# A recurrent attention kernel with its segment loop rebuilt: four column tiles, shared leftover rows, 12 of 32 weight slabs streamed

## The chip, the cores and the metric

The kernel runs on one core of one Trainium2 chip. The metric is the device time in microseconds. The time before is 4046.12 us (median of 3 runs, 4042.35 to 4054.03).

Names used below: PE is the matmul engine (PEld its loads of the stationary operand), DVE the vector engine, ACT the scalar engine, POOL the general-purpose engine; SP only issues DMAs here. A "q" behind an engine's name (ACTq) means its instruction queue. HBM is the memory off the chip. A column tile is a strip of columns of PE's array (32 or 64 here, `tile_position` in the code) with a stationary operand of its own. To evict is to copy a result out of the matmuls' accumulators. The granted clock is the share of full speed that the records give PE; they know only 1.0 (full) and 0.5 (half).

## The reference

The output is the sum of three things over 2048 rows of width 1024. The first is the input itself. The second is a dense block (1024 to 3584 with a gelu, back to 1024) on the normalised rows. The third is attention in segments of 32 rows that carries 8 memory rows along:

```python
for s in range(n_seg):                       # 64 segments, one after another
    xs = x[:, s * seg_len:(s + 1) * seg_len, :]
    h = concatenate([mem, xs], axis=1)       # 8 memory rows + 32 rows
    q, k, v = h @ Wq, h @ Wk, h @ Wv         # 1024 -> 32 heads x 128
    p = softmax(where(mask, q @ k.T * scale, -1e9))
    o = (p @ v) @ Wo                         # 4096 -> 1024
    mem = o[:, :8, :]                        # the next segment needs these
    outs.append(o[:, 8:, :])
```

Each of Wq, Wk, Wv and Wo is 8 MiB in bf16. Neither kernel keeps all 32 MiB on chip (18 MiB before, 20 after); the rest is read again from HBM in each of the 64 segments. The loop is serial: the memory rows of one segment come out of the Wo product of the one before.

One caution on correctness. Every run below agreed with the reference within the comparison's tolerance. So did an experiment that used wrong weights on purpose (`nostream`). The attention term is evidently small beside the other two, so agreement says little about the recurrent part. The experiments other than `nostream` and `fill` change only the order, place or time of the same operations; `fill` adds zeros.

## The kernel before

The dense part keeps all of w1 and w2 on chip and runs in four groups of 512 rows.

The segment loop keeps Wq, Wk and a quarter of Wo on chip. Q and K use the weights as the stationary operand, with 40 moving columns. V uses the 40 rows of `h` as the stationary operand, O the 40 rows of the attention's result, both in two column tiles, with Wv and three quarters of Wo streamed in blocks of 1 MiB:

```python
for i, h in enumerate(range(g0, g1)):                  # Q and K
    for kt in range(KT):
        nc.tensor.matmul(pv[:, i, :], lhsT=W_sb[:, kt, h*DH:(h+1)*DH], rhs=hT[:, kt, :], ...)

for kq in range(KT // 4):                              # V; O is alike
    blk = spool.tile([P, 4, 1024], BF16, name="wblk")
    nc.sync.dma_start(out=blk, in_=Wv_v[...])          # 1 MiB
    for kk in range(4):
        nc.tensor.matmul(psA[0:L, :],     lhsT=hT[:, kt, :], rhs=blk[:, kk, 0:512],    tile_position=(0, 0))
        nc.tensor.matmul(psB[QB:QB+L, :], lhsT=hT[:, kt, :], rhs=blk[:, kk, 512:1024], tile_position=(0, QB))
```

The softmax here doesn't subtract the row's maximum and nothing guards it: scores larger than these inputs give would overflow.

## Time and profile before

| stage | from the trace |
|---|---|
| dense matmuls | 54.6 to 502.5 us |
| 64 segments | one per 54.4 us (mean spacing of the output stores), 14 MiB streamed in each |

First some lines of the page of the kernel before: engines with busy time and share, the granted clock in tenths per fortieth of the span, the DMA share in the same slices, and the chain that ended last.

```profile
PE 3026.4 (75%) x48265; PEld 1854.1 (46%) x48265; DVE 871.5 (22%) x1764; ACT 1020.1 (25%) x1561; POOL 9.9 (0%) x23
...
PEclk9999967777777787777787777777777777777777
DMA  4000097787777777877777787777787777778776
...
PE 55%; DMA 24%; ACT 8%; issue 7%; DVE 6%; SPq 1%; ACTq 0%; DVEq 0%
```

Next, groups of instructions from the same page (line, engine, operation, tiles, shapes, count, then busy us, mean ns and the idle time before them with its releaser), and the line of the largest DMA issue (size of one, us to landing).

```profile
L373 PE MATMUL ps<-wblk,oT 128*40 128x512 bf16 x1536 | 657.0, 578 | 297.4 <-DMA wblk<-in_A_Wo_dram 296.5
...
L266 PE MATMUL ps<-hT,Wk_sb 128*128 128x40 bf16 x16384 | 485.1, 188 | 177.3 <-issue 177.2
...
wblk<-in_A_Wv_dram SPq DMA_DIRECT2D x512, 1024.0 KB, 8.7
```

No engine is full. PE is busy 75% of the span, at a clock of seven to eight tenths in the loop, and 24% of the chain is DMA. A third view gives one stretch of the loop: busy time of PE, its weight loads, DVE, ACT and POOL, then the granted clock, the DMA share and GB/s.

```profile
600.00:4000.00 3400.00, 2531.75 (x45112) 1622.27 (x45108) 653.97 (x1185) 824.16 (x1243) 0.00 (x0) 0.78 0.77 275
```

The queue that feeds the loop has a share of 0.77. In stretches where it is full (share 1.0 and more) it moved 369 to 397 GB/s with 2 KB rows, so about a quarter of its time is lost.

### The profile page before, as it was taken

What the parts mean: (1) busy time and instruction counts of PE and PEld (TensorE: products, weight loads), DVE (VectorE), ACT (ScalarE), POOL (GpSimd) and SP (SyncE); (2) the same over time, 40 slices, a digit from 0 to 9 for tenths busy, and PEclk for the clock granted to TensorE, in tenths of its full rate; (3) what the DMA queues carried; (4) which work ended last, traced back from release to release, by engine and by line L of the source; (5) the groups of instructions that cost most, each with busy time, mean ns of one, the idle gap of its engine ahead of it and who ended that gap; (6) DMA issues with size and microseconds to landing.
All of it is one profiled execution on the core that took longest, in us unless ns stands there. A gap on an engine that the chain in (4) does not pass through costs nothing.

```text
span 4043.0 us, 102945 instructions
## 1 busy us (share of the span) xinstructions
PE 3026.4 (75%) x48265; PEld 1854.1 (46%) x48265; DVE 871.5 (22%) x1764; ACT 1020.1 (25%) x1561; POOL 9.9 (0%) x23
## 2 busy tenths in 40 slices
PE   5999937777777777777777777777777777777777
PEld 2444424444454544444544444445444444544444
DVE  4343302112112211121122111212112112211211
ACT  3333312122222222222222122222122222212222
POOL 0000000000000000000000000000000000000000
PEclk9999967777777787777787777777777777777777
DMA  4000097787777777877777787777787777778776
GB/s 172 32 32 27 12 347 250 272 292 278 269 282 260 276 274 285 296 282 259 282 265 265 277 296 275 264 268 271 262 290 284 277 274 266 263 270 293 281 275 247
DMA packets 502262, 1004.93 MB, mean 249 GB/s; under 512 B 20035, under 2 KB 28227, under 8 KB 499788
## 3 DMA queue, kind: packets, MB, share of 16 engines
q1 hardware_dynamic: 494396, 985.74, 67.8%
q8 instruction: 377, 6.18, 0.6%
q10 hardware_dynamic: 6160, 8.41, 0.6%
q0 software_dynamic: 1280, 4.20, 0.3%
q14 instruction: 49, 0.40, 0.0%
HBM read 985.69 MB, written 12.58 MB: 247 GB/s over the span
## 4 chain that ended last, share of the span: by engine, by line
PE 55%; DMA 24%; ACT 8%; issue 7%; DVE 6%; SPq 1%; ACTq 0%; DVEq 0%
PE ps L266 23%; DMA wblk<-in_A_Wo_dram 18%; PE ps L288 9%; PE ps L373 9%; PE ps L181 4%; DMA wblk<-in_A_Wv_dram 4%; PE ps L154 3%; PE ps L292 2%; PE ps L312 2%; ACT L340 2%; ACT L339 2%; ACT rsum L340 1%; ACT pack L296 1%; ACT rsum L339 1%; DVE pack L387 1%
## 5 line engine op out<-in xcount | busy, mean ns | idle before, releaser
L373 PE MATMUL ps<-wblk,oT 128*40 128x512 bf16 x1536 | 657.0, 578 | 297.4 <-DMA wblk<-in_A_Wo_dram 296.5
L288 PE MATMUL ps<-wblk,hT 128*40 128x512 bf16 x2048 | 595.3, 443 | 138.5 <-DVE hT L247 88.5
L377 PE MATMUL ps<-wblk,oT 128*40 128x512 bf16 x1536 | 664.7, 584 | 0.0
L266 PE MATMUL ps<-hT,Wk_sb 128*128 128x40 bf16 x16384 | 485.1, 188 | 177.3 <-issue 177.2
L292 PE MATMUL ps<-wblk,hT 128*40 128x512 bf16 x2048 | 595.8, 443 | 6.1 <-issue 6.1
L296 ACT CAST pack<-ps 40x512 bf16<-40x512 f32 x256 | 147.0, 574 | 1786.0 <-PE ps L292 1665.3
L266 PEld LDWEIGHTS <-Wk_sb 128*128 128x128 bf16 x16384 | 472.9, 101 | 183.8 <-issue 183.8
L266 PEld LDWEIGHTS <-Wq_sb 128*128 128x128 bf16 x16384 | 442.9, 98 | 149.2 <-issue 149.2
L266 PE MATMUL ps<-hT,Wq_sb 128*128 128x40 bf16 x16384 | 461.6, 183 | 65.8 <-issue 65.8
L377 PEld LDWEIGHTS <-oT 128*40 128x40 bf16 x2048 | 240.8, 134 | 413.3 <-issue 412.8
L373 PEld LDWEIGHTS <-oT 128*40 128x40 bf16 x2048 | 270.0, 136 | 340.6 <-issue 309.0
L288 PEld LDWEIGHTS <-hT 128*40 128x40 bf16 x2048 | 212.1, 111 | 331.0 <-issue 176.2
L297 DVE CAST pack<-ps 40x512 bf16<-40x512 f32 x256 | 177.4, 693 | 547.7 <-PE ps L292 492.2
L382 DVE CAST pack<-ps 8x512 bf16<-8x512 f32 x64 | 43.8, 685 | 934.5 <-PE ps L377 934.5
L276 DVE CAST kT<-ps 128x440 bf16<-128x440 f32 (+1 forms) x128 | 76.2, 595 | 740.8 <-PE ps L266 740.8
L292 PEld LDWEIGHTS <-hT 128*40 128x40 bf16 x2048 | 212.4, 111 | 31.7 <-issue 7.4
L181 PE MATMUL ps<-w_sb,gT 128*128 128x512 bf16 x896 | 204.0, 385 | 9.8 <-DVE gT L173 9.8
L154 PE MATMUL ps<-xnT,w_sb 128*128 128x512 bf16 x896 | 200.9, 389 | 3.1 <-DVE xnT L148 3.1
L344 PE MATMUL ps<-expT,pack 40*128 40x40 bf16 x2048 | 75.8, 181 | 167.7 <-ACT pack L296 167.7
L373 PE MATMUL ps<-Wo_res,oT 128*40 128x512 bf16 x512 | 201.0, 563 | 0.0
L377 PE MATMUL ps<-Wo_res,oT 128*40 128x512 bf16 x512 | 200.5, 563 | 0.0
L351 DVE TENSOR_TENSOR oT<-ps,rsum 128x480 bf16<-128x480 f32 (+1 forms) x192 | 109.7, 599 | 300.1 <-ACT rsum L340 297.0
(61 smaller groups left out, 1973.6 us busy)
## 6 DMA issues: line engine op xcount, KB each, us to landing
wblk<-in_A_Wv_dram SPq DMA_DIRECT2D x512, 1024.0 KB, 8.7
wblk<-in_A_Wo_dram SPq DMA_DIRECT2D x384, 1024.0 KB, 8.8
Wq_sb<-in_A_Wq_dram SPq DMA_DIRECT2D x8, 1024.0 KB, 13.9
Wk_sb<-in_A_Wk_dram SPq DMA_DIRECT2D x8, 1024.0 KB, 19.9
w_sb<-in_B_w_dram SPq DMA_DIRECT2D x8, 896.0 KB, 10.4
w_sb<-in_B_w_dram SPq DMA_DIRECT2D x7, 1024.0 KB, 15.6
xtok<-in_A_x_dram SPq DMA_DIRECT2D x16, 256.0 KB, 2.7
xnbuf<-ln_xn POOLq DMA_DIRECT2D x16, 256.0 KB, 2.3
```

Source lines behind the costliest of these rows:

```text
L154: nc.tensor.matmul(ps[:, :], lhsT=w1_sb[:, kt, fb * P:(fb + 1) * P], rhs=xnT[:, kt, :], start=(kt == 0), stop=(kt == KT - 1),)
L181: nc.tensor.matmul(ps[:, :], lhsT=gT[:, fc, tt * P:(tt + 1) * P], rhs=w2_sb[:, fc, cs], start=(fc == 0), stop=False,)
L266: nc.tensor.matmul(pv[:, i, :], lhsT=W_sb[:, kt, h * DH:(h + 1) * DH], rhs=hT[:, kt, :], start=(kt == 0), stop=(kt == KT - 1),)
L288: nc.tensor.matmul(psA[0:L, :], lhsT=hT[:, kt, :], rhs=blk[:, kk, 0:512], start=(kt == 0), stop=(kt == KT - 1), tile_position=(0, 0),)
L292: nc.tensor.matmul(psB[QB:QB + L, :], lhsT=hT[:, kt, :], rhs=blk[:, kk, 512:1024], start=(kt == 0), stop=(kt == KT - 1), tile_position=(0, ...
L296: nc.scalar.copy(out=V[0:L, csA], in_=psA[0:L, :])
L297: nc.vector.tensor_copy(out=V[0:L, csB], in_=psB[QB:QB + L, :])
L339: nc.scalar.activation(out=rs[:, 0:n * L], in_=pss_l[g][:, 0:n * L], func=ACT.Ln)
L340: nc.scalar.activation(out=rs[:, 0:n * L], in_=rs[:, 0:n * L], func=ACT.Exp, scale=-1.0)
L351: nc.vector.tensor_tensor(out=oT[:, h0:h1, :], in0=pv, in1=rs[:, 0:n * L].rearrange("p (f c) -> p f c", c=L), op=ALU.mult,)
L373: nc.tensor.matmul(psO_A[0:L, :], lhsT=oT[:, ki, :], rhs=blk[:, kk, 0:512], start=first, stop=last, tile_position=(0, 0),)
L377: nc.tensor.matmul(psO_B[QB:QB + L, :], lhsT=oT[:, ki, :], rhs=blk[:, kk, 512:1024], start=first, stop=last, tile_position=(0, QB),)
```

## The change

The recurrent part is rewritten, with three aims. PE should use four column tiles of 32 rows in each projection. A segment has 40 rows, so a pass takes 24 rows of the segment and the 8 memory rows; the 8 leftover rows (`hL`) of four segments are put together into one more pass, once in four segments for Q, K and V, and once for O. And only 12 of the 32 MiB should be streamed, three slabs of 1 MiB from each of the four weights, 20 staying resident. The dense part is adapted to a new memory layout, and the whole kernel is now scheduled by hand: instructions run on each engine in the order in which they are written.

```diff
+NX = 24
+NL = SEG - NX
+GRP = 4
+RES = {"K": 5, "Q": 5, "V": 5, "O": 5}
+STREAM_BUFS = 4
...
+    ctx.enter_context(tc.manual_schedule())
...
             for fb in range(FC):
...                              # the same six gelu operations, in this order on each engine
+    def units(w):
+        for i in range(NSLAB):
+            for u in range(2):
+                if i < RES[w]:
+                    t = res_tiles[(w, i)][:, 2048 * u:2048 * u + 2048]
+                else:
+                    st = stp.tile([P, 2048], BF16, name="st")
+                    ... nc.sync.dma_start(out=st, ...)             # 0.5 MiB
+                    t = st[:, :]
+                yield i, u, t
...
+    for s in range(NSEG):
+        g, i4 = divmod(s, GRP)
+        if i4 == 0:
+            hL = sp.tile([P, KT, SEG], BF16, name="hL", bufs=2)
+            nc.scalar.dma_start(out=hL[:, :, :], in_=xL_d[:, g, :]...)
...
+            for i, u, t in units(w):                               # K, Q, V
+                for lhs, acc in ((hT, ps), (hL, psL)):             # psL only if i4 == 0
+                    for j in range(4):
+                        nc.tensor.matmul(acc[32*j:32*j+32, u, :], lhsT=lhs[:, i, :],
+                                         rhs=t[:, 512*j:512*j+512], tile_position=(0, 32*j), ...)
+                if mid is not None and (i, u) == (3, 1):
+                    mid()                                          # transposes of the pass before
...                              # scores, Exp, sums, Ln, Exp, PV, then O with units("O")
+        if i4 == GRP - 1:
+            resL = sp.tile([P, 256], BF16, name="resL")
+            nc.scalar.dma_start(out=resL, in_=RL_d[g]...)
+            nc.vector.tensor_tensor(out=otL, in0=psXL[:, 0:256], in1=resL, op=ALU.add)
+            for jq in range(4):
+                for i in range(GRP):
+                    nc.scalar.dma_start(out=rows[i, NX:SEG, ...], in_=otL[...])     # 16 stores
```

A unit is one half slab, that is 2048 columns of weights, four matmuls (in O eight of 256 columns). A pass is 16 units: ten resident ones, then six streamed ones.

## The prediction

> **What bounds it now.** The dense part ends near 503 us; then 64 segments, one per 54.6 us (spacing of output stores in the timeline). A segment is a serial loop, mixed in the chain of waits: PE 55%, DMA 24%, ACT 8%, issue 7%. It streams 14 MiB. In saturated 4 us windows the queue moves 388 GB/s with 2 KB rows (2.70 us per MiB), about 420 with 8 KB rows; the stage averages 276 GB/s, DMA share 0.77. Q/K matmuls with their 128-column loads take about 14 us. Projection pairs start every 0.215 us at full clock, 0.425 at half: two column tiles run fully together. Mean granted clock is 0.78; the clock records step in 3.41 us between 1.0 and 0.5 only. After a half-clock window under about 70% busy it stays half; after a full one under about 50% it drops. The Trainium skill ("TensorE: Matmul & The Clock Gate", Part 1) also has two states and 3.4 us windows; the trace agrees.
>
> **What changes.**
> 1. Streaming falls to 12 MiB, in 4 KB rows (2 KB for Wo): about 31.5 us a segment, a floor.
> 2. Each projection unit (2048 weight columns) is four 512-column matmuls in four column tiles. The skill's "TensorEngine Tiling (Array Packing)", Theoretical Speedup, allows up to 4x; before shows 2x. I assume 0.215/0.43 us per unit: a pass of 16 units is 3.4 to 6.9 us.
> 3. One segment in four runs Q, K, V twice, another O twice.
> 4. Four table loads of 1.28 us go. But softmax is exposed: no V pass lies in it. Last V unit to oT ready: scores 2, exp 0.7, sums 0.4, Ln and Exp 1.1, multiplies 0.7, PV 2, copies 0.9: 8 to 9 us with hops.
> 5. Dense part: starts after the first weight slice instead of at 54.6 us (saves 30 us), loses 64 matmuls of 0.215 us (14 us), pays some in layernorm gaps. Then 11 MiB of slabs load exposed, 29 us instead of about 60. First segment near 488 us.
>
> **Critical path.** Streamed units come last in each pass (10 resident, then 6 streamed), with four 0.5 MiB buffers: 5.3 us of prefetch, refilled only when consumed, about 2 us after issue. At full clock, residents and transposes take 3 us, the queue never empties, a pass costs 8 us (DMA); attention plus O 17; segment 41 us. At half clock residents take over 5 us, the queue runs dry, a pass costs 10 us; segment 52, doubled ones 57 to 73. Waiting for the stream keeps PE mostly at half clock, so I expect about 52 us averaged, 45 if mostly full.
>
> **Prediction.** 488 + 64 x 52 = about 3820 us; range 3450 to 4150. Faster by over 2%: 0.68; within 2%: 0.18; slower: 0.14.
>
> **What would show each step.** 805 MB streamed in the loop; DMA share 0.6 to 0.75, dips in attention and at pass starts. Four-tile groups 0.215/0.43 us apart. Mean clock 0.6 to 0.75. PE's largest wait on the streamed buffer, in every pass. No table loads inside segments. Exposed chain after V of 8 to 10 us. Segments with doubled Q, K, V longest by about 10 us. Dense matmuls starting near 25 us.
>
> **What would make it wrong.** Four tiles not overlapping (0.43 us at full clock: 60 us or more a segment); 256-column O matmuls bound by loads; a clock that stays full (about 3400 us); "issue" stalls like the 4 us a segment before; DMA issue on ACT (0.31 to 0.36 us each) delaying evictions.

## More of the kernel before

A last view, the timeline of the dense part, shows one gelu block; the columns are start, duration, engine, line, operation, tiles, shapes, and in brackets the idle time before and what ended it.

```profile
201.15 0.69 ACT L162 ACTIVATE g_xb<-ps,b1col 128x512 bf16<-128x512 f32 x1 [0.69 <-DVE gT L173]
201.74 0.62 ACT L172 ACTIVATE g_sg<-g_u 128x512 bf16<-128x512 bf16 x1
201.87 0.42 DVE L166 TENSOR_TENSOR g_u<-g_xb 128x512 bf16<-128x512 bf16 x1 [0.48 <-ACT g_xb L162]
...
203.05 0.69 ACT L162 ACTIVATE g_xb<-ps,b1col 128x512 bf16<-128x512 f32 x1 [0.69 <-DVE gT L173]
```

The bias activation (g_xb) comes every 1.90 us. The sigmoid (g_sg) follows it at once because it belongs to the previous block: its input was ready at 201.39, before this bias activation had ended.

One gelu block looks as follows; its emission order is rearranged by the scheduler of the framework.

```python
for fb in range(FC):                                   # 28 blocks of 128 columns
    ... 8 matmuls into ps ...
    nc.scalar.activation(out=xb, in_=ps, func=ACT.Identity, bias=b1col[:, fb:fb + 1])
    nc.vector.tensor_tensor(out=u, in0=xb, in1=xb, op=ALU.mult)
    nc.vector.tensor_scalar(out=u, in0=u, ...)
    nc.vector.tensor_tensor(out=u, in0=u, in1=xb, op=ALU.mult)
    nc.scalar.activation(out=sg, in_=u, func=ACT.Sigmoid, scale=GELU_C)
    nc.vector.tensor_tensor(out=gT[:, fb, :], in0=sg, in1=xb, op=ALU.mult)
```

## The result, and the profile after

The time after is 4218.78 us (median of 4 runs, 4201.1 to 4233.11) against 4046.64 us in the same rounds: the ratio is 1.0417, with a 95% interval of 1.038 to 1.0454. Ratios here are the mean time of one kernel's runs over that of the other's of the same rounds, so they are not quite the ratios of the medians quoted. The kernel is slower, and the predicted range of 3450 to 4150 us does not hold it.

The same lines of the page, for the kernel after:

```profile
PE 2541.1 (60%) x37359; PEld 1224.6 (29%) x37379; DVE 628.7 (15%) x1419; ACT 545.7 (13%) x1032; POOL 33.8 (1%) x92
...
PEclk9889877676776777777677776767777777667677
DMA  4100247666675757575756666666757575757566
...
PE 46%; DMA 36%; ACT 6%; DVE 5%; issue 3%; ACTq 3%; SPq 0%; POOL 0%; DVEq 0%; POOLq 0%
```

```profile
L363 PE MATMUL acc<-st,hT 128*32 128x512 bf16 x4608 | 453.4, 429 | 751.6 <-DMA st<-in_A_Wq_dram 254.5
...
L363 PE MATMUL acc<-WK,hL 128*32 128x512 bf16 x640 | 81.0, 498 | 188.8 <-DMA hL<-xL_d 188.8
...
st<-in_A_Wk_dram SPq DMA_DIRECT2D x384, 512.0 KB
```

```profile
700.00:4200.00 3500.00, 2042.76 (x34500) 1004.59 (x34499) 351.07 (x778) 382.15 (x761) 24.44 (x61) 0.72 0.65 229
```

PE is busy for 485 us less. The loop streams 12 MiB instead of 14. And yet the DMA share fell from 0.77 to 0.65 and the rate from 275 to 229 GB/s. The work was taken away, and the time was not. The chain has become more of a DMA chain, 36% instead of 24%, while the queue is less used. PE is idle 751.6 us ahead of the streamed matmuls of K, Q and V, and 188.8 us ahead of the first matmuls on hL.

One plain segment in the timeline of PE shows how that comes about:

```profile
2021.86 3.65 PE L363 MATMUL acc<-WQ,hT 128*32 128x512 bf16 x32
2025.45 0.85 PE L329 MATMUL tr<-ident,nat 128*128 128x128 bf16 x8
2026.23 0.61 PE L363 MATMUL acc<-WQ,hT 128*32 128x512 bf16 x8
2026.67 0.82 PE L363 MATMUL acc<-st,hT 128*32 128x512 bf16 x12
2028.22 0.40 PE L363 MATMUL acc<-st,hT 128*32 128x512 bf16 x4 [0.73 <-DMA st<-in_A_Wq_dram]
2030.46 0.40 PE L363 MATMUL acc<-st,hT 128*32 128x512 bf16 x4 [1.84 <-DMA st<-in_A_Wq_dram]
2032.50 0.40 PE L363 MATMUL acc<-st,hT 128*32 128x512 bf16 x4 [1.64 <-DMA st<-in_A_Wq_dram]
2032.72 3.58 PE L363 MATMUL acc<-WV,hT 128*32 128x512 bf16 x32
```

This is the Q pass. Eight resident units take 3.65 us, then come the transposes, two more residents, and three streamed units that were already there. Then PE waits for the fourth, fifth and sixth streamed unit. Units in four-tile groups of 0.43 us are the half clock. The groups do overlap: `nostream` below has them 0.21 us apart at full clock.

What the queue did meanwhile is seen in windows of the same segment: the resident part of Q, its streamed part, and the resident part of O (columns as in the windows above).

```profile
2021.86:2026.67 4.81, 4.81 (x52) 2.20 (x48) 1.02 (x2) 1.16 (x2) 0.00 (x0) 0.57 0.92 342
2026.67:2032.72 6.05, 1.84 (x29) 0.72 (x24) 0.09 (x1) 0.01 (x1) 0.00 (x0) 1.00 0.73 251
...
2049.39:2053.40 4.01, 4.01 (x80) 2.98 (x84) 0.30 (x2) 0.12 (x1) 0.00 (x0) 0.52 0.00 0
```

While PE works through the residents of Q, the queue refills the four buffers (share 0.92). It stands still once they are full, until PE has used a streamed unit and the next load has started: in Q, K and V for a short time. In O it is otherwise. The buffers are filled again during the attention, and through O's residents the queue moves nothing. Over all 30 plain segments behind the first group (length less DMA share times length) the queue stands still for 13.0 of 49.1 us: 5.8 in O, 2.4 in K, 2.1 each in Q and V, 0.6 in the attention. For 36.1 us it is busy.

The start of a group of four segments shows something else. The timeline of the last segment of a group, ACT's queue and the first matmuls on PE:

```profile
1934.04 1.69 ACTq L507 DMA_DIRECT2D out_dram<-ot  x4
1935.77 0.36 ACTq L512 DMA_DIRECT2D resL<-RL_d  x1
...
1939.05 5.48 ACTq L518 DMA_DIRECT2D out_dram<-otL  x16
1944.57 0.36 ACTq L348 DMA_DIRECT2D hL<-xL_d  x1
...
1946.56 0.62 PE L363 MATMUL acc<-WK,hL 128*32 128x512 bf16 x4 [12.32 <-DMA hL<-xL_d]
```

ACT issues its DMAs in the order in which they are written. The load of resL is issued at 1935.77, an addition waits for it until 1938.59, and the 16 leftover stores are issued, 0.34 us each. Only then, at 1944.57, does the load of hL go out that the next segment needs for its second group of matmuls. PE waits 12.32 us for it. In the list of waits this is one line, 15 times in 64 segments:

```profile
PE sm L492 <- DMA st<-in_A_Wo_dram: 266.8, 128, 3.7
...
PE acc L363 <- DMA st<-in_A_Wq_dram: 251.6, 173, 4.3
...
PE acc L363 <- DMA hL<-xL_d: 188.8, 15, 13.8
```

And the gelu blocks in the dense part:

```profile
190.48 0.67 ACT L233 ACTIVATE g_xb<-ps,b1col 128x512 bf16<-128x512 f32 x1
...
192.48 0.63 ACT L243 ACTIVATE g_sg<-g_u 128x512 bf16<-128x512 bf16 x1 [1.34 <-DVE g_u L241]
193.02 0.67 ACT L233 ACTIVATE g_xb<-ps,b1col 128x512 bf16<-128x512 f32 x1
...
195.57 0.67 ACT L233 ACTIVATE g_xb<-ps,b1col 128x512 bf16<-128x512 f32 x1
```

The bias activation now comes every 2.54 us. The sigmoid waits 1.34 us for DVE, since it belongs to the same block. So ACT waits for DVE once in each block, and DVE waits for ACT twice (0.76 us for the sigmoid, 0.15 for the bias activation). The dense matmuls run from 27.4 to 578.5 us, instead of 54.6 to 502.5.

The following table is worked out from the traces. A segment is counted from the transposes of its memory rows to those of the next. "Group start" are the segments with double K, Q and V, "group end" those with double O, "plain" the two between. The first group is left out of these three columns.

| kernel | time, us | first segment at | group start | plain | group end | mean |
|---|---|---|---|---|---|---|
| after | 4218.78 | 596.1 | 75.9 | 49.1 | 51.1 | 56.3 |
| hl_early | 4046.63 | 595.8 | 64.9 | 49.2 | 51.7 | 54.0 |
| gelu_pipe | 4100.66 | 508.1 | 75.5 | 48.4 | 51.7 | 56.0 |
| hlgelu | 3971.26 | 509.0 | 65.0 | 49.0 | 51.4 | 53.8 |
| hlgeluact | 3935.59 | 507.9 | 61.9 | 49.3 | 51.9 | 53.3 |
| fill | 4239.32 | 594.6 | 73.9 | 50.5 | 53.2 | 57.0 |
| after_b5n | 3902.76 | 596.3 | 69.2 | 44.6 | 47.1 | 51.4 |
| spread | 3662.94 | 596.5 | 58.5 | 43.5 | 44.7 | 47.7 |
| all3 | 3517.20 | 506.2 | 55.5 | 43.6 | 45.3 | 47.1 |
| best5 | 3366.47 | 507.7 | 53.6 | 40.3 | 43.5 | 44.5 |
| best6 | 3208.58 | 507.6 | 42.6 | 40.5 | 43.6 | 41.9 |
| best7 | 3200.16 | 507.1 | 41.9 | 40.2 | 43.8 | 41.7 |
| nostream | 2414.80 | 508.7 | 45.1 | 22.9 | 27.0 | 29.5 |

### The profile page after: what moved, and what is told of

It reads as the page before. It is cut to its first block, busy times and chain, and to the rows that moved or that the text cites. A ratio compares the mean times of both kernels' runs of the same rounds, so it can differ in the third digit from the quotient of the medians.

```text
span 4204.2 us, 82534 instructions
## 1 busy us (share of the span) xinstructions
PE 2541.1 (60%) x37359; PEld 1224.6 (29%) x37379; DVE 628.7 (15%) x1419; ACT 545.7 (13%) x1032; POOL 33.8 (1%) x92
## 4 chain that ended last, share of the span: by engine, by line
PE 46%; DMA 36%; ACT 6%; DVE 5%; issue 3%; ACTq 3%; SPq 0%; POOL 0%; DVEq 0%; POOLq 0%
PE acc L363 24%; PE sm L492 10%; DMA st<-in_A_Wk_dram 9%; DMA st<-in_A_Wq_dram 9%; DMA st<-in_A_Wv_dram 8%; DMA st<-in_A_Wo_dram 7%; PE ps L258 4%; PE tr L329 2%; ACTq L518 2%; ACT g_xb L233 2%; PE ps L225 1%; DMA resL<-RL_d 1%; DVE g_u L241 1%; DVE g_u L237 1%; ACT oT L477 1%
## 5 line engine op out<-in xcount | busy, mean ns | idle before, releaser
L363 PE MATMUL acc<-st,hT 128*32 128x512 bf16 x4608 | 453.4, 429 | 751.6 <-DMA st<-in_A_Wq_dram 254.5
L363 PEld LDWEIGHTS <-hT 128*32 128x32 bf16 x12288 | 417.9, 119 | 1467.9 <-issue 1315.1
L492 PEld LDWEIGHTS <-oT 128*32 128x32 bf16 x8192 | 282.6, 127 | 418.8 <-issue 301.5
L492 PE MATMUL sm<-WO,oT 128*32 128x256 bf16 x5120 | 309.3, 389 | 47.1 <-ACT oT L477 45.3
L492 PE MATMUL sm<-st,oT 128*32 128x256 bf16 x3072 | 168.7, 325 | 266.8 <-DMA st<-in_A_Wo_dram 266.8
L363 PE MATMUL acc<-WK,hT 128*32 128x512 bf16 x2560 | 281.5, 573 | 25.0 <-DVE hT L315 18.1
L363 PE MATMUL acc<-WV,hT 128*32 128x512 bf16 x2560 | 279.6, 546 | 17.9 <-DVE nat L322 17.9
L363 PE MATMUL acc<-WQ,hT 128*32 128x512 bf16 x2560 | 280.0, 548 | 15.8 <-DVE nat L322 15.8
L225 PE MATMUL ps<-xnT,w 128*128 128x512 bf16 x896 | 212.3, 393 | 33.8 <-ACT g_xb L233 30.6
L258 PE MATMUL ps<-w,gT 128*128 128x512 bf16 x876 | 205.3, 392 | 36.4 <-DVE gT L244 32.7
L363 PE MATMUL acc<-WK,hL 128*32 128x512 bf16 x640 | 81.0, 498 | 188.8 <-DMA hL<-xL_d 188.8
```

What stands on the lines that cost most here:

```text
L225: nc.tensor.matmul(ps[:, :].rearrange("p (s t) -> p s t", t=SEG), lhsT=w1_sb[fb // 4][:, kt, (fb % 4) * P:(fb % 4 + 1) * P], rhs=xnT[:, :, ...
L258: nc.tensor.matmul(ps[:, :], lhsT=gts[fc // 7][:, fc % 7, tt * P:(tt + 1) * P], rhs=w2_sb[fc // 4][:, fc % 4, cs], start=(fc == 0), stop=( ...
L363: nc.tensor.matmul(acc[32 * j:32 * j + 32, u, :], lhsT=lhs[:, i, :], rhs=t[:, 512 * j:512 * j + 512], start=(i == 0), stop=(i == NSLAB - 1 ...
L492: nc.tensor.matmul(acc[32 * jq:32 * jq + 32, 0:256], lhsT=lhs[:, 4 * c + j, :], rhs=t[:, 1024 * k + 256 * jq:1024 * k + 256 * jq + 256], s ...
```

## The experiments

My theory after the result had three parts: the late load of hL, the gelu blocks in which ACT and DVE wait for each other, and streamed units bunched at the end of a pass. A rival for the third was the clock: PE waits, falls to half clock, and is late for that reason.

### hl_early: the leftover rows loaded two segments earlier

```diff
             if i4 == 0:
-                hL = sp.tile(...); nc.scalar.dma_start(out=hL, in_=xL_d[:, g, :]...)
+                hL = hL_next
+            if i4 == 1 and g + 1 < NGRP:
+                hL_next = load_hl(g + 1)
```

> The one change against the kernel after: the leftover rows (hL) of the next group of four segments are loaded two segments early instead of behind the sixteen output stores on ACT's queue. Theory: PE sat idle 12.6 us for hL at the start of 15 segments (188.8 us in the waits of the kernel after), nothing else covers it, so the time falls by about 180 us, from about 4215 to about 4035 us, and the wait on hL disappears. Rival: the K pass of these segments is bound by the stream or by PE anyway and the wait only moves to the streamed buffers; then the time falls by less than 60 us.

Measured: 4046.63 us, ratio to before 1.0009 (0.9982 to 1.0037). That is 172 us below the median of after, close to the 180 expected. No wait on hL is left, and the group-start segment fell from 75.9 to 64.9 us. This one misplaced load is worth the whole difference between "slower" and "the same".

### gelu_pipe: the next bias activation ahead of this sigmoid

```diff
             for fb in range(FC):
                 ... matmuls into ps ...
                 nc.scalar.activation(out=xb, in_=ps, func=ACT.Identity, ...)
-                u = ...; sg = sigmoid(u); gT[fb] = sg * xb            # of this block
                 ... # xb now has four buffers instead of two
+                if held is not None:
+                    done = gelu_rest(*held)                           # u, sigmoid of block fb-1
+                    if last is not None:
+                        gelu_end(*last)                               # product of block fb-2
+                    last = done
+                held = (fb, xb)
```

> The one change against the kernel after: in the dense part the bias activation of block fb+1 is emitted ahead of the sigmoid of block fb, so that ACT does not wait for DVE inside each block. Theory: one block costs 2.54 us in the kernel after because ACT and DVE wait for each other in turn; the busy times alone (ACT 1.3, DVE 1.6, PE 1.73 us) allow 1.75 to 1.9 us, so 112 blocks save 70 to 90 us: about 4130 us. Rival: the dense part is long because of layernorm gaps and the stores of R_d on ACT's queue; then less than 25 us is saved.

Measured: 4100.66 us, ratio 1.0139 (1.0115 to 1.0163), 118 us below after. The dense matmuls end at 490.4 instead of 578.5 us, which is 88 us, as expected; the medians differ by 30 us more, and the loop of this run is shorter by 0.3 us a segment (20 us) for no reason that I tested. In the new timeline the bias activation comes every 1.73 us, the time of PE's own eight matmuls.

### spread: streamed units interleaved with resident ones

```diff
-    for i in range(NSLAB):
-        for u in range(2):
+    for i, u in ORDER:      # R R S R S R R S R S R R S R S R: same units, same buffers
```

> The one change against the kernel after: the same 6 streamed and 10 resident units of a pass, but interleaved (R R S R S R R S R S R R S R S R) instead of all resident first. Theory: with the streamed units at the end of a pass the four buffers are full and the queue stands still while PE works through residents, attention included; interleaved, a buffer comes free every 0.5 to 1 us, the queue is nearly always busy, and a plain segment falls from about 49.5 us to 36 to 42 us: 3550 to 3750 us in all, DMA share in the loop above 0.8. Rival: the passes are slow because the queue delivers 4 KB rows slowly or because PE runs at half clock; then the order of the units matters little and the time stays above 4000 us.

Measured: 3662.94 us, ratio 0.9055 (0.9034 to 0.9076), 556 us below after. The time expected was met. The plain segment was not: 43.5 us, not 36 to 42. The windows of the loop, for spread:

```profile
700.00:3100.00 2400.00, 1512.94 (x27898) 772.10 (x27902) 283.86 (x629) 309.01 (x615) 19.62 (x49) 0.80 0.78 271
```

The DMA share went from 0.65 to 0.78, just short of the 0.8 expected, and the rate from 229 to 271 GB/s, with the same bytes per segment. In a plain segment the queue is busy for 36.6 us, as in after (36.1), and stands still for 6.9 instead of 13.0. No work was removed; only the order was changed. The clock rose with it, from 0.72 to 0.80, so this run alone does not part the two.

### fill: extra matmuls to keep PE busy while it waits

```diff
+    if (i, u) in FILL_AT:                  # ahead of the last three streamed units
+        for _ in range(3):
+            for j in range(4):
+                nc.tensor.matmul(ps[32*j:32*j+32, u, :], lhsT=zero, rhs=res_tiles[(w, 0)][...],
+                                 start=False, stop=False, tile_position=(0, 32*j))
```

> The one change against the kernel after: ahead of the last three streamed units of each K, Q and V pass PE does three extra units of matmuls with zero weights (they add zero), about 0.65 us each time at full clock, so that it is busy while it waits for the stream. Theory of the clock: PE drops to half clock because it waits, residents then take 4 us instead of 2.2, the buffers are refilled late; with fill the mean granted clock in the loop rises from 0.72 to above 0.85 and a plain segment falls from 49.5 by 3 to 6 us although PE does more: 3850 to 4050 us in all. Rival: the clock does not matter since the bunched stream sets the pass; then the time stays the same or rises by up to 200 us.

Measured: 4239.32 us, ratio 1.0467 (1.0427 to 1.0506), 21 us above after. The clock in the loop rose only from 0.72 to 0.79, so the dose was too small for a clean test. Where it did act it can be read: the ten residents of Q and V ran at a clock of 0.77 and 0.83 instead of 0.59 and 0.61, and took 3.62 and 3.35 us, transposes included, instead of 4.40 and 4.29. Under one microsecond per pass is what that share of the clock was worth, and the extra matmuls cost more. What the residents gained came back as waiting and extra work ahead of the streamed units: the Q and V passes of a plain segment took 11.3 and 10.9 us; in after they took 11.2 and 10.7. I take the clock for a second-order cause here; the run suggests it and does not prove it. That a clock held at full throughout would not pay is not shown.

### after_b5n: one more stream buffer, the order unchanged

```diff
-STREAM_BUFS = 4
+STREAM_BUFS = 5
-            V = sp.tile([P, 1024], BF16, name="V")
+            V = sp.tile([P, 1024], BF16, name="nat", bufs=2)      # makes room
```

> Against the kernel after: five stream buffers instead of four, and V in one of the rotating nat buffers to make room; the order (residents first) is unchanged. Theory: what hurts in that order is that the queue stands still with full buffers; one more buffer of 0.5 MiB is 1.28 us more of prefetch per pass, of which most is saved in each of four passes: a plain segment falls by 3 to 6 us, 3820 to 4030 us in all. Rival: what helped in spread was only that PE no longer idles long enough to lose its clock; then one buffer more saves under 80 us.

Measured: 3902.76 us, ratio 0.9636 (0.9607 to 0.9665), 316 us below after. A plain segment fell by 4.5 us, inside the 3 to 6 expected, but not evenly: Q became 1.9 us shorter, V 1.0, O 1.8, and K 0.3 us longer. So the saving of 1.28 us in every pass, as the theory had it, is not what happened. What did happen is that the queue was busy for as long as in after (36.3 us of a plain segment) and stood still for 8.3 us instead of 13.0. The rival allowed 80 us, and 316 were saved. The clock is not quite out of it: it rose from 0.72 to 0.76 in the loop, and in the residents of V from 0.62 to 0.92. In fill a clock of 0.82 there did not make the V pass shorter, though fill's own matmuls stand in that pass too.

### nostream: no weight streamed in the loop, wrong result

```diff
+    if i >= RES[w]:
+        t = res_tiles[(w, i - 3)][:, 2048 * u:2048 * u + 2048]
```

It also has the edits of hl_early and gelu_pipe.

> Wrong result on purpose. The kernel after with the early hL load and the reordered gelu, and in which every unit that was streamed reads a resident slab instead (slab i-3), so that no weight is streamed in the loop. It shows what the serial loop costs without the stream: 12 resident-like units more per segment, PE never waiting on st. Theory: the stream is what a plain segment of 49 us waits for; without it PE stays dense, the clock goes to full, and a plain segment takes 4 x 3.5 to 4 us of units plus 5 us of attention and 1.5 us of hops, so 21 to 25 us; 1850 to 2150 us in all. Rival: the serial chain of evictions, transposes and softmax is as long as the stream; then a plain segment stays above 35 us.

Measured: 2414.80 us, ratio 0.5963 (0.5934 to 0.5992), above the 2150 us expected. The plain segment of 22.9 us is as expected; the group-start segment of 45.1 us is what I had not counted. So the serial work of a plain segment is 23 us (at nearly full clock), the stream alone 31.5 us at the rates of before, or 36 us by the queue's busy time in after, and the kernel after takes 49. With a DMA share of 0.65 the queue stood still for a good third of the loop. Two lines of PE's timeline also settle the four column tiles:

```profile
1501.70 1.91 PE L387 MATMUL acc<-WQ,hT 128*32 128x512 bf16 x32
1503.44 1.90 PE L387 MATMUL acc<-WV,hT 128*32 128x512 bf16 x32
```

Each line is eight units, 32 matmuls of 512 columns, in 1.9 us with the tail of the last: one group of four every 0.21 us, the time of one such matmul in before.

### all3: the three edits together

```diff
 hl_early + gelu_pipe + spread
```

> The three mends together (hL early, gelu reordered, streamed units interleaved). If the three causes are independent the savings add: 4215 - 168 - 115 - 552 = about 3380 us, within 3340 to 3420 us. If late hL hides stream time that now shows (the queue fills while PE waits for hL), it is 3420 to 3500 us.

Measured: 3517.20 us, ratio 0.8679 (0.8642 to 0.8715). That misses 3380 us by 137 and lies just above the range I gave for "late hL hides stream time". The group-start segment still took 55.5 us, only 3 less than in spread. The list of waits names the reason:

```profile
ACT nat L339 <- DMA out_dram<-otL: 274.2, 15, 19.1
...
PE acc L388 <- DVE nat L340: 162.2, 45, 10.7
```

With hL early, PE finishes the doubled K pass sooner, and then ACT is not there. It is still held by resL and the 16 stores, so it cannot evict K, and Q waits for the accumulators. The same queue had a second victim, hidden behind the first.

### best5: all3 with five stream buffers

```diff
 all3 + STREAM_BUFS = 5, V in a nat buffer
```

> all3 with five stream buffers (V in a nat buffer). Theory: in the interleaved order the queue still stands still for 3 to 4 us in the softmax of each segment, and a fifth buffer fills 1.3 us of it; 40 to 100 us less than all3. Rival: the interleaved order is already bound by the rate of the queue; then it is within 20 us of all3.

Measured: 3366.47 us, ratio 0.8310 (0.8289 to 0.8331), 151 us below all3, more than the 40 to 100 expected. A plain segment fell by 3.3 us, more than the 1.3 us of one softmax. Of this, 2.6 us are in the O pass, behind the softmax, and 0.8 in V; K and Q did not become shorter.

### best6: ACT's queue relieved

```diff
+            if i4 == GRP - 1:                       # at the start of the segment
+                resL = ...; nc.scalar.dma_start(out=resL, in_=RL_d[g]...)
...
-                        nc.scalar.dma_start(out=rows[i, NX:SEG, ...], in_=otL[...])
+                        nc.gpsimd.dma_start(out=rows[i, NX:SEG, ...], in_=otL[...])
```

> best5 with ACT's queue relieved at the end of each group: resL is loaded at the start of the group's last segment, and the sixteen leftover stores go out on POOL's queue. Theory: in all3 and best5 loading hL early gained little because ACT was still held by these sixteen issues, so that the K eviction of the next segment waited for them (ACT nat on DMA out_dram<-otL, 274 us in 15 waits in all3) and Q waited for the eviction; then the group-start segment falls from 53.6 to about 44 to 47 us, 100 to 150 us in all: 3220 to 3270 us. Rival: that segment is long because PE does K, Q, V twice; then less than 40 us is saved.

Measured: 3208.58 us, ratio 0.7911 (0.7884 to 0.7937), 158 us below best5, a little more than the 100 to 150 expected. The two halves of the edit were not tried apart. The group-start segment fell from 53.6 to 42.6 us, two more than a plain one, although it does K, Q and V twice. The wait of ACT on the leftover stores is gone from the list. The rival, that the doubled passes themselves are long, falls for this kernel.

### best7: another interleaving

```diff
-    R R S R S R R S R S R R S R S R
+    S R R S R R S R R S R R S R S R
```

> best6 with another interleaving, one streamed unit first and then one after every two residents (S R R S R R S R R S R R S R S R). Theory: the buffers that filled up during the softmax are given back one unit earlier, so the queue restarts sooner: 20 to 60 us less than best6. Rival: the exact order does not matter once the units are spread: within 15 us of best6.

Measured: 3200.16 us, ratio 0.7904 (0.7878 to 0.7930), 8 us from best6 and inside its scatter. The rival holds: once the units are spread, the exact order is of no account. The windows of its loop:

```profile
700.00:3100.00 2400.00, 1622.40 (x32048) 855.04 (x32041) 327.49 (x725) 357.50 (x711) 138.14 (x283) 0.84 0.89 311
```

The queue is at 0.89 and 311 GB/s. This is the fastest kernel, 21% below before and 24% below after.

### hlgelu and hlgeluact: only the two slips mended

```diff
 hlgelu    = hl_early + gelu_pipe                    (streamed units last, four buffers)
 hlgeluact = hlgelu + the edit of best6
```

> The kernel after with only the two slips mended that the prediction had not seen: hL loaded early, gelu reordered; streamed units still last, four buffers. Theory: these two are what separates the prediction from the result; savings add to 4215 - 168 - 115 = about 3930 us (3890 to 3970), the first segment starts near 508 us as predicted within 20 us, and a segment averages 53 to 54 us. Rival: mending one uncovers another wait, as in all3; then it stays above 3990 us.

> hlgelu with resL loaded early and the sixteen leftover stores on POOL's queue. Theory: in the residents-first order the K pass of a group-start segment ends about 17 us after its start, later than the 14 us for which ACT is held, so this gains little: within 40 us of hlgelu. Rival: ACT's queue holds up the evictions here too; then 80 us or more is saved.

Measured: hlgelu 3971.26 us, ratio 0.9823 (0.9773 to 0.9872), so faster than before, though whether by 2% is unclear, and one microsecond above the range given; hlgeluact 3935.59 us, ratio 0.9706 (0.9667 to 0.9745), 36 us less, as expected. In hlgelu the first segment starts at 509.0 us and a segment takes 53.8 us in the mean, both within the numbers expected. The two savings add up to 248 us instead of 290; the loops differ by tenths of a microsecond per segment from run to run, and I did not settle where the 42 us are.

## Why the prediction was wrong

**The step that failed first was item 5**, "Dense part: starts after the first weight slice instead of at 54.6 us (saves 30 us), loses 64 matmuls of 0.215 us (14 us), pays some in layernorm gaps ... First segment near 488 us." It started at 27.4 us, as forecast ("near 25 us"). But it ended at 578.5 us, and the first segment began at 596.1, 108 us late. The diff leaves the gelu operations as they were, and I costed them as in before. What had changed was the line `manual_schedule`: the order in the source became the order on the engine. gelu_pipe undid that and the first segment began at 508.1 us. So 88 of the 108 us are the gelu order; the other 20 were mis-sized.

**The second failing step was the critical path of the segment**, in which I had every load in time and only the streamed units late. "DMA issue on ACT (0.31 to 0.36 us each) delaying evictions" stood among the risks, with the right duration, but I did not follow ACT's queue across the end of a group. What it delayed first was a load, hL: 12.6 us in 15 segments, 188.8 us in all, about 2.95 us per segment in the mean. Evictions came second, as all3 showed.

**The rest was a matter of size.** I took 52 us as the mean segment; hlgelu, with the two slips mended, has 53.8. One term that was too small is the "floor" of item 1, 31.5 us of streaming in a segment: the queue is busy for 36 to 38 us of a plain segment in every kernel here that streams. Another is "doubled Q, K, V longest by about 10 us": the group-start segment is 27 us longer than a plain one in after, 16 in hl_early, where hL no longer waits. Together: 4204 us measured in the profile, less 3820, is 384 us. Of these 108 are the later first segment, 189 the wait for hL, and about 87 remain as 1.4 us per segment.

**What was right.** The standing queue was named as the mechanism, with its numbers: a pass of about 10 us at half clock was 10.2 to 11.2 us (means of K, Q and V), a plain segment of 52 us was 49.1, DMA share 0.65 (forecast 0.6 to 0.75), mean clock 0.72 (0.6 to 0.75), no table load inside a segment, the largest waits on the streamed buffers in every pass. Spread and after_b5n confirm it by two different means: the queue's busy time stays and its standing time falls. Some luck is in the 49.1: 52 less three passes of 10 leaves 22 us for attention and O, which took 16.3, and K, Q and V took 32.1 instead of 30. Dips were forecast "in attention and at pass starts"; in the attention the queue is busy for 4.6 of 5.2 us, and its long stop is at the start of O. Four tiles overlapped fully: the Trainium skill, "TensorEngine Tiling (Array Packing)", Theoretical Speedup, allows up to 4 times for 32 columns, and the trace of nostream agrees with 0.21 us per group. I gave the clock more weight than fill supports.

**What was off in the other direction.** The exposed chain from the last V unit to the first O matmul was forecast as 8 to 9 us and took 5.1. The term was the scores ("scores 2") and PV: I priced 64 small matmuls at the 30 to 37 ns of before, and in four tiles they started 8 ns apart, 0.51 us for all; the PV matmuls took 0.51 us as well instead of 2.

**Where the expected gain went.** Before and after differ little in the loop, 54.4 and 56.3 us per segment, although 2 MiB of stream, the Q and K weight loads and the table loads are gone. It turned into new waits. The old loop spread its V passes between Q, K and softmax, so that buffers were given back at several points of a segment. The new one gives no buffer back while PE works through ten residents, and then six close together. Interleaving alone brings the mean segment to 47.7 us; with hL early, a fifth buffer and ACT's queue relieved as well, best6 is at 41.9 and best7 at 41.7.

**Left open.** In the fastest kernel the queue is at 311 GB/s at a share of 0.89, and in a plain segment it stands still for only 3.9 of 40.2 us; why the bytes per busy time are lower than in the full stretches of before was not tested. The 20 to 40 us by which savings did not add were not settled.

## What to carry to other kernels

Bytes streamed per iteration say little until you have asked at which moments the buffers are given back. If resident and streamed operands alternate, a small ring of buffers keeps the queue going; if the residents come first, the same ring stands full for part of each pass, most of all behind a stretch (here the attention) that uses none of it. When a change takes scheduling into its own hands, read every engine's queue as one line in source order, across the loop's edge too: a DMA that the next iteration needs must not stand behind stores that wait for this one.

## What the Trainium skill lacked or had wrong

- "DMA: Bandwidth & Descriptors", section "Issuing engines are not separate DMA queues", says that starting DMAs from several engines only saves the time to initiate them, usually small relative to the DMA. Here that time was not small: 16 stores of 4 KiB held ACT for 5.48 us, and with the wait ahead of them they kept PE waiting 12.32 us for a load, and in all3 they held up an eviction. Moving the stores to POOL's queue and loading resL early was worth 158 us (best6).
- "TensorE: Matmul & The Clock Gate", Part 1, agrees with the trace that there are two clock states and windows of 3.4 us. Its table has the clock fall after an idle window. In the loop of after (640 to 4200 us) windows with much less idle time did it: of 214 windows at full clock in which PE was busy 10 to 40% of the time, the next was at half clock in all 214; at 40 to 50% in 33 of 63, above 50% in none of 175. Back to full it went after none of 284 windows busy under 70%, after 13 of 69 at 70 to 80%, and after all 236 above 80%. The upper edge differs by kernel: in the loop of before (640 to 4040 us), 29 of 67 full windows busy 50 to 70% were followed by half clock. (Busy is the union of the matmuls' recorded times.)
- The same page and part ("Wait — 56ns, not 53.3ns?") has a floor of about 25 ns between starts of small matmuls. The 64 score matmuls of a segment, in four column tiles, start 8 ns apart in the mean. Taken by tile, that is every fourth matmul, the starts are at least 24 ns apart and 33 in the mean, so here the floor holds within a tile and not across four; the passage does not say this.
- No page gives the order of streamed and resident operands within a pass; the nearest is the general advice to interleave regimes in "Perfetto Trace Analysis", Optimization Strategy. Interleaving them was worth 556 us of 4219 here.
